# Seven block products in place of eight in the first layer of three expert visits

## The chip, the cores and the metric

The kernel runs on one core of one Trainium2 chip. The metric is the device time of one execution in microseconds (us). The core has a matrix engine (TensorE, PE), VectorE (DVE), ScalarE (ACT), GpSimd (POOL) and the queue of SyncE (SP) that issues the transfers.

## The reference

```python
def reference(**kwargs):                                   # shortened
    attn = top32_attention(q, k, v)                        # 2 x 8 heads x 576 x 64
    x = attn.transpose(0, 2, 1, 3).reshape(1152, 512)
    # first mixture: every token goes through every expert
    logits = x @ w_gate; P = np.exp(logits - logits.max())
    for _ in range(8):                                     # Sinkhorn
        P /= P.sum(1, keepdims=True) + 1e-09
        P /= P.sum(0, keepdims=True) + 1e-09
        P *= N / E
    for e in range(8):
        out += P[:, e:e + 1] * (np.maximum(x @ w1[e], 0.0) @ w2[e])   # w1: 512 x 1024, w2: 1024 x 512
    # second mixture: each token goes to the expert of its largest logit, capacity 288
    return moe2(out, ...)
```

All inputs and the output are float32. The change concerns the first mixture alone, and in it the product `x @ w1[e]` of some tokens and experts.

## The kernel before

The 1152 tokens lie transposed in SBUF (`xt`, 512 features in four chunks `d` of 128 partitions, one column for a token) and are cut into nine tiles of 128. Every float32 operand of a fast matmul is split in two parts: a rounding (`h`) that ScalarE makes and a remainder (`l`), a difference that VectorE or GpSimd makes. A product is then three matmuls: h by h, h by l, l by h.

A *visit* `(e, t0, t1)` takes expert `e` over the tiles `t0` to `t1 - 1`. It goes through eight *hidden blocks* of 128 hidden units. For each, `weights()` loads a block of w1 (`ra`) and of w2 (`rb`) and splits both (L975 on ScalarE; the remainder at L981 on GpSimd in early visits, at L978 on VectorE in late ones). The first layer (L1041) is 12 matmuls with as many columns as the visit has tokens, summed in one PSUM bank; `parts()` makes the Relu and its rounding (L989, ScalarE) and the remainder (L991, VectorE); the second layer (L1153) is three matmuls of 512 columns for each tile, summed over the eight hidden blocks in one bank a tile. At the end of a visit an early one parks its tiles in DRAM (L1142, L1144), and a late one multiplies them by the Sinkhorn weights and adds them to `acc` (`combine()`, L1175 and L1178). `restore()` brings the parked ones back (L1188) through the three buffers `ys` and `yt`, and adds them in the same way.

The visits in `EARLY` are interleaved with attention. When attention is over, `turn_over()` frees its memory and makes the late buffers; the job is called `gate` (its copy is L359). From there `sinkhorn()` runs: eight rounds, each with four small VectorE operations on rows (L1212 to L1215: a reduce, a TENSOR_SCALAR, a reciprocal, a TENSOR_TENSOR), a TensorE matmul that sums over partitions (L1225), and four on columns (L1218 to L1221, of the same kinds). The visits in `LATE` follow: three of 512 columns (experts 5, 6 and 7 over tiles 2 to 5), one of 256 columns (expert 2 over tiles 4 and 5), and eight *whole* ones of 384 columns (tiles 6 to 8). A whole visit makes all eight hidden blocks first and then the second layer tile by tile, with its own buffers for hidden blocks (`h_last`, cut from `ff`) and for w2 (`w2_last`, cut from `v`). Meanwhile tiles whose sum is finished are routed for the second mixture (`route_all()`, L1706 to L1781).

The order on each engine is fixed when the program is built. `Order` keeps a clock for each engine; every job has a rank and an estimated cost, and an engine takes the job that can start first, the lowest rank among those that can start within 0.02 us. Each engine then runs its list in that order and waits, in it, for what a job depends on. The ranks that matter here are:

```python
R = -2000                            # sinkhorn, every engine
rank - 1.5, rank                     # PE: first layer, second layer (rank = 1000 + unit)
-1000 + k * 0.001                    # ACT, DVE: Relu, remainder of a hidden block
-500 + rank, -100 + rank             # ACT: rounding of weights; DVE or POOL: remainder
-50, 10                              # restored outputs: DVE add, SP load
```

There are eight PSUM banks; in the late part five belong to the pool `psm` (hidden blocks and output tiles) and three to `psa`.

Of the kernel before, what the change touches and what calls it, by code (L numbers as in the profile page):

```python
# [219 lines left out]
class Net:  # L220
# [971 lines left out]
    def sinkhorn(self):  # L1192
# [39 lines left out]
        self.restore()  # L1232

    def made_late(self, mem):
# [9 lines left out]
        n = 4 * self.cap  # L1244
        cut = [v[:, i * n:(i + 1) * n].rearrange("p (d c) -> p d c", d=4) for i in range(4)]
        self.over = [cut[:2], cut[2:]]
        self.rest = v[:, 4 * n:]
        flat = self.ff.rearrange("p a b -> p (a b)")
        cut = [flat[:, i * self.DM:(i + 1) * self.DM] for i in range(12)]
        self.end_ = [cut[i:i + 2] for i in range(0, 12, 2)]  # L1250
# [579 lines left out]
```

## Time and profile before

| | |
|---|---|
| median of 3 runs | 1176.47 us (1176.34 to 1177.87) |
| profiled execution | 1177.07 us, span of its instructions 1175.2 us |
| PE, DVE, ACT, POOL busy in the span | 1151.5, 907.2, 729.5, 440.5 us |
| granted TensorE clock | 0.998 of 2.4 GHz |
| HBM traffic | 165 GB/s over the span |

The span runs from the first to the last instruction. Matmuls are pipelined, so two that follow each other overlap in the records, and the pace is read from starts, not from durations. An engine's waits are put down to what ended last before it went on.

### The profile page before, as it was taken

How to read it: one execution, taken by the hardware profiler on the slowest of the kernel's cores; microseconds unless marked ns; L12 is line 12 of the kernel's file. 1: busy time of each engine (PE TensorE's matmuls, PEld its weight loads, DVE VectorE, ACT ScalarE, POOL GpSimd, SP SyncE). 2: the span in 40 equal slices, each digit the busy share in tenths (PEclk: the TensorE clock that was granted, in tenths of full speed). 3: DMA queues.
4: the chain of work that ended last, by engine and by line, in shares of the span. 5: the costliest groups of instructions: out<-in, count | busy, mean ns of one | idle time of the engine just before them, and what ended most of it. 6: DMA issues, size and time to landing. Idle time of an engine off the chain costs nothing.

```text
span 1175.2 us, 20867 instructions
## 1 busy us (share of the span) xinstructions
PE 1151.5 (98%) x6607; PEld 1005.3 (86%) x6607; DVE 907.2 (77%) x2178; ACT 729.5 (62%) x1731; POOL 440.5 (37%) x403
## 2 busy tenths in 40 slices
PE   8999999999999999999999999999999999999997
PEld 5877888888889888888888888989999999898886
DVE  7998999999999999998655567844555555568882
ACT  7666889888788877768543334543334444258882
POOL 5466877777556744547500000100000000016541
PEclk9999999999999999999999999999999999999999
DMA  5467666655444655536555555643444444279980
GB/s 141 110 173 204 200 182 186 190 167 156 138 134 111 201 164 148 164 109 187 153 184 175 161 171 155 204 135 114 130 125 144 144 131 136 75 238 358 344 273 23
DMA packets 243607, 195.08 MB, mean 166 GB/s; under 512 B 67551, under 2 KB 186335, under 8 KB 243488
## 3 DMA queue, kind: packets, MB, share of 16 engines
q1 hardware_dynamic: 241232, 188.78, 53.8%
q0 software_dynamic: 1648, 4.73, 1.0%
q8 instruction: 54, 0.88, 0.3%
q14 instruction: 65, 0.53, 0.2%
q10 hardware_dynamic: 608, 0.15, 0.1%
HBM read 172.87 MB, written 21.33 MB: 165 GB/s over the span
## 4 chain that ended last, share of the span: by engine, by line
PE 54%; DVE 31%; ACT 6%; issue 5%; DMA 2%; POOL 1%; SPq 0%; POOLq 0%; DVEq 0%; ACTq 0%
PE yp L1041 14%; PE yp L1153 12%; PE tp L1153 8%; DVE wk L773 7%; PE tp L1041 6%; DVE m L775 6%; DVE e L784 3%; DVE hl L991 2%; DVE m L769 2%; PE yp L1372 2%; DVE wk L719 2%; DVE etl L830 2%; DVE m L721 1%; PE tp L264 1%; PE tp L1388 1%
## 5 line engine op out<-in xcount | busy, mean ns | idle before, releaser
L1781 POOL DMA_INDIRECT disp<-acc,idx x9 | 10.3, 1141 | 436.7 <-DVE run L1777 436.7
L981 POOL TENSOR_TENSOR w0l<-ra,w0h 128x512 fp32r<-128x512 f32 x104 | 134.8, 1296 | 95.0 <-ACT w0h L975 88.3
L981 POOL TENSOR_TENSOR w1l<-rb,w1h 128x512 fp32r<-128x512 f32 x104 | 134.7, 1296 | 49.8 <-ACT w1h L975 45.6
L975 ACT ACTIVATE w0h<-ra 128x512 fp32r<-128x512 f32 x211 | 131.9, 626 | 0.0
L775 DVE MAX8 m<-wk 128x8 f32<-128x576 f32 x168 | 125.0, 751 | 1.1
L975 ACT ACTIVATE w1h<-rb 128x512 fp32r<-128x512 f32 x148 | 93.3, 630 | 52.3 <-PE yp L1153 41.3
L1041 PE MATMUL yp<-xh,w0h 128*128 128x256 f32 (+2 forms) x528 | 107.2, 325 | 0.3 <-DVE hl L991 0.2
L1041 PE MATMUL yp<-xl,w0h 128*128 128x256 f32 (+2 forms) x528 | 106.7, 324 | 0.0
L1041 PE MATMUL yp<-xh,w0l 128*128 128x256 f32 (+2 forms) x528 | 106.6, 323 | 0.0
L1153 PE MATMUL yp<-w1h,hh 128*128 128x512 f32 x240 | 98.0, 408 | 0.4 <-DVE hl L991 0.4
L989 ACT ACTIVATE hh<-yp 128x256 fp32r<-128x256 f32 (+3 forms) x113 | 49.6, 439 | 76.3 <-PE yp L1041 60.0
L1041 PEld LDWEIGHTS yp<-xh,w0h 128*128 128x128 f32 x528 | 87.7, 188 | 10.1 <-DVE hl L991 1.6
L1153 PE MATMUL yp<-w1l,hh 128*128 128x512 f32 x240 | 94.2, 393 | 0.0
L1153 PE MATMUL yp<-w1h,hl 128*128 128x512 f32 x240 | 94.1, 392 | 0.0
L975 ACT ACTIVATE v<-rb 128x512 fp32r<-128x512 f32 x65 | 40.5, 629 | 79.5 <-PE yp L1153 41.8
L991 DVE SCALAR_TENSOR_TENSOR hl<-yp,hh 128x256 fp32r<-128x256 f32 (+3 forms) x113 | 55.2, 488 | 44.2 <-ACT hh L989 43.7
L1041 PEld LDWEIGHTS yp<-xh,w0l 128*128 128x128 f32 x528 | 85.1, 189 | 3.8
L1041 PEld LDWEIGHTS yp<-xl,w0h 128*128 128x128 f32 x528 | 85.0, 189 | 3.9
L1153 PE MATMUL yp<-v,f 128*128 128x512 f32 x360 | 84.4, 391 | 0.0
L773 DVE MATCH_REPLACE8 wk<-m,wk 128x576 f32<-128x576 f32 x112 | 83.2, 743 | 0.4
L1153 PEld LDWEIGHTS yp<-v,f 128*128 128x128 f32 x360 | 67.2, 188 | 13.5
L978 DVE TENSOR_TENSOR w0l<-ra,w0h 128x512 fp32r<-128x512 f32 x107 | 73.5, 687 | 0.4
(555 smaller groups left out, 3026.2 us busy)
## 6 DMA issues: line engine op xcount, KB each, us to landing
rb<-in_moe_w_dram SPq DMA_DIRECT2D x248, 256.0 KB, 3.0
ra<-in_moe_w_dram SPq DMA_DIRECT2D x245, 256.0 KB, 3.1
acc<-in_moe_w_dram SPq DMA_DIRECT2D x67, 256.0 KB, 6.0
y<-ys SPq DMA_DIRECT2D x33, 256.0 KB, 2.4
ys<-y SPq DMA_DIRECT2D x23, 256.0 KB, 3.0
vr<-in_v_dram SPq DMA_DIRECT2D x40, 128.0 KB, 2.8
disp<-z SPq DMA_DIRECT2D x6, 771.0 KB, 5.0
qg<-in_q_dram SPq DMA_DIRECT2D x63, 64.0 KB, 2.6
```

The lines of the kernel that those rows point to most:

```text
L719: j = self.job("DVE", r, 0.73, lambda i=i: nc.vector.match_replace(wk.t, m.t[:, i], flat() if i == 0 else wk.t, LOW), deps=[j], take=[wk] ...
L769: j = j0 = self.job("DVE", r, 0.66, lambda: nc.vector.max(m.t[:, 0], flat()), deps=got, take=[m])
L773: j = self.job("DVE", r, 0.73, lambda i=i: nc.vector.match_replace(wk.t, m.t[:, i], flat() if i == 0 else wk.t, LOW), deps=[j], take=[wk] ...
L775: j = self.job("DVE", r, 0.66, lambda i=i: nc.vector.max(m.t[:, i + 1], wk.t), deps=[j], use=[wk] if i == 2 else [])
L784: masks.append(self.job("DVE", r, t_dve(288) + 0.08, lambda half=half, p=p: nc.vector.scalar_tensor_tensor(e.t[:, half * 288:(half + 1) * ...
L975: jh = self.job("ACT", -500 + rank, t_act(512, True), lambda r=r, w=w: nc.scalar.activation(w.t[0], r.t, AF.Copy), deps=[j], take=[w])
L978: jl = self.job("DVE", -100 + rank, t_dve(512, True), lambda r=r, w=w: nc.vector.tensor_sub(w.t[1], r.t, w.t[0].bitcast(F32)), deps=[jh], ...
L981: jl = self.job("POOL", -100 + rank if k > 8 * NATIVE + 4 else FIRST - 3, t_pool(512), lambda r=r, w=w: nc.gpsimd.tensor_sub(w.t[1], r.t, ...
L989: jh = self.job("ACT", -1000 + k * 0.001, t_act(b - a), lambda: nc.scalar.activation(h.t[0][:, a:b], p.t[:, :b - a], AF.Relu), deps=deps, ...
L991: jl = self.job("DVE", -1000 + k * 0.001, t_dve(b - a), lambda: nc.vector.scalar_tensor_tensor(h.t[1][:, a:b], p.t[:, :b - a], 0.0, h.t[0] ...
L1041: nc.tensor.matmul(p.t[:, :b - a], w1[0].t[i][:, d, :], self.xt[s][:, d, c0 + a:c0 + b], start=m == 0 and d == 0, stop=m == 2 and d == 3)
L1153: nc.tensor.matmul(y[t].t, h.t[i][:, c:c + 128], w2[0].t[s], start=f == 0 and m == 0, stop=f == last and m == 2)
```

## The change

The three visits of experts 5, 6 and 7 over tiles 2 to 5 become `visit_seven()`. It takes hidden blocks in pairs. The first layer of a pair is a product of a 2 by 2 arrangement of weight blocks (two hidden blocks by two halves of the 512 features) with a 2 by 2 arrangement of tokens (two halves of the features by two halves of 256 columns). Strassen's scheme, in Winograd's form, makes the four results from seven block products. Each product is 6 matmuls of 256 columns (three for the two parts, by two chunks). The sums of weight blocks S1 to S4 are made by GpSimd for every pair, then rounded by ScalarE (L975's form) and given a remainder by VectorE. The sums of token blocks are made once, in `halves()`, by ten GpSimd operations of 512 columns, four ScalarE roundings and four GpSimd remainders. The products go to four banks; banks that are summed further are copied in between by ScalarE (`snap`), and four VectorE operations add or subtract a bank and a copy; Relu and remainder then read the copy in SBUF.

The visit of expert 2 over tiles 4 and 5 is moved ahead of these three, and `restore()` is set up after it. The buffers of the whole visits (`ff`, `v`) are made only when the last of the three is done (`made_last()`), in the memory of the buffers of `visit_seven()` (`mid`).

```diff
--- before.py
+++ after.py
@@ -25,7 +25,8 @@
 WITH = 3
 FILL = 390.0
 EARLY = [(0, 0, 1), (1, 0, 1)] + [(e, 0, 2) for e in range(2, 8)] + [(0, 1, 4), (1, 1, 4), (2, 2, 4), (3, 2, 6), (4, 2, 6), (0, 4, 6), (1, 4, 6)]
-LATE = [(5, 2, 6), (6, 2, 6), (7, 2, 6), (2, 4, 6)] + [(e, 6, 9) for e in (2, 3, 4, 5, 6, 7, 0, 1)]
+SEVEN = [(5, 2, 6), (6, 2, 6), (7, 2, 6)]
+LATE = [(2, 4, 6)] + SEVEN + [(e, 6, 9) for e in (2, 3, 4, 5, 6, 7, 0, 1)]
 ALONE = 16
 FIRST = 16
 ROWS = 16
@@ -1008,8 +1009,14 @@
                 self.visit(*v, early=True)
 
     def late_one(self):
+        self.halves()
         for v in LATE[:-1]:
+            if v in SEVEN:
+                self.visit_seven(*v)
+                continue
             self.visit(*v, whole=v[2] - v[1] == 3)
+            if v == LATE[0]:
+                self.restore()
         self.visit(*LATE[-1], whole=True)
         seen = sorted((e, t) for e, a, b in EARLY + LATE for t in range(a, b))
         assert seen == [(e, t) for e in range(self.E) for t in range(self.NT)]
+    def halves(self):
+
+        nc, c0, n = self.nc, 256, 256
+        b = self.sums_.box()
+        x = [[[self.xt[s][:, 2 * i:2 * i + 2, c0 + k * n:c0 + k * n + n] for k in (0, 1)] for i in (0, 1)] for s in (0, 1)]
+        self.cut_x = x
+        f = lambda s, a, z: x[s][a][z].bitcast(F32)
+
+        made = [d for t in range(2, 6) for d in self.xdone[t]] + [self.gate]
...
+        def step(eng, fn, deps, take=()):
+            e = nc.vector if eng == "DVE" else nc.gpsimd
+            cost = t_dve(512, True) if eng == "DVE" else t_pool(512)
+            return self.job(eng, -99.0, cost, lambda: fn(e), deps=deps, take=take, use=[b])
...
+        j = step("POOL", sub(r[0], g(0, 0, 1), g(0, 0, 0)), made, take=[b])
+        j3 = step("POOL", sub(r[2], g(0, 1, 1), g(0, 0, 1)), made + [j])
+        j3 = step("POOL", sub(r[3], g(1, 1, 1), g(1, 0, 1)), [j3])
+        j3 = step("POOL", add(r[2], r[2], r[3]), [j3])
+        j = step("POOL", sub(r[4], g(1, 0, 1), g(1, 0, 0)), [j])
+        j1 = step("POOL", add(r[0], r[0], r[4]), [j])
+        j = step("POOL", sub(r[1], g(0, 1, 1), r[0]), [j1])
+        j2 = step("POOL", add(r[1], r[1], g(1, 1, 1)), [j])
+        j = step("POOL", sub(r[3], r[1], g(0, 1, 0)), [j2, j3])
+        j4 = step("POOL", sub(r[3], r[3], g(1, 1, 0)), [j])
+        self.halved = []
+        for i, j in enumerate((j1, j2, j3, j4)):
+            jh = self.job("ACT", -600, t_act(512, True), lambda i=i: nc.scalar.activation(self.tt[0][:, i], room(i), AF.Copy),
+                          deps=[j], use=[b])
+            jl = self.job("POOL", -99.5, t_pool(512), lambda i=i: nc.gpsimd.tensor_sub(
+                self.tt[1][:, i], room(i), self.tt[0][:, i].bitcast(F32)), deps=[jh], use=[b])
+            self.halved += [jh, jl]
+
+    def visit_seven(self, e, t0, t1):
+
+        nc, fb, y, n = self.nc, self.F // 128, {}, 256
+        banks = [self.psm.box(), self.psm.box()]
+        for f in range(0, fb, 2):
+            pair = f // 2
...
+            k, rank = self.unit, 1000 + self.unit
+            self.unit += 2
+            raw, loads, w2 = [], [], []
+            for m in range(2):
+                r, cut = self.r7.box(), slice((f + m) * 128, (f + m + 1) * 128)
+                loads.append(self.job("SP", 20 + 0.001 * (k + m), 0.45, lambda r=r, cut=cut: nc.sync.dma_start(
+                    r.t, self.w11[e, :, cut].rearrange("(c p) n -> p c n", p=128)), take=[r], lag=1.35))
+                raw.append(r)
+            ra, rb = raw
+            a, q = self.seven.box(), self.sums_.box()
+            R = -98 + 0.001 * k
+            def pool(fn, deps, take=(), ra=ra, rb=rb, a=a, q=q):
+                return self.job("POOL", R, t_pool(256), lambda: fn(nc.gpsimd, ra.t, rb.t, q.t), deps=deps, take=take, use=[ra, rb, q])
+            g = self.gate
+            js = pool(lambda v, x, z, o: v.tensor_add(o[:, 0], z[:, 0:2], z[:, 2:4]), loads + [g], [q])
+            js = pool(lambda v, x, z, o: v.tensor_sub(o[:, 1], o[:, 0], x[:, 0:2]), [js])
+            js = pool(lambda v, x, z, o: v.tensor_sub(o[:, 2], x[:, 0:2], z[:, 0:2]), [js])
+            js = pool(lambda v, x, z, o: v.tensor_sub(o[:, 3], x[:, 2:4], o[:, 1]), [js])
+            fine = []
...
+                    (3, 7, lambda q=q: q.t, [js], q))):
+                w = (hi - lo) * 256
+                jh = self.job("ACT", -500 + 0.001 * k, t_act(w, True), lambda a=a, lo=lo, hi=hi, part=part: nc.scalar.activation(
+                    a.t[0][:, lo:hi], part(), AF.Copy), deps=deps, take=[] if m else [a], use=[a, box])
+                jl = self.job("DVE", -100 + 0.001 * k, t_dve(w, True), lambda a=a, lo=lo, hi=hi, part=part: nc.vector.tensor_sub(
+                    a.t[1][:, lo:hi], part(), a.t[0][:, lo:hi].bitcast(F32)), deps=[jh], use=[a, box])
+                fine.append([jh, jl])
...
+            p = [banks[pair]] + [self.psa.box() for _ in range(3)]
+            c = [pool_.box() for pool_ in self.taken]
+            order = ((0, A11, old(0, 0), True), (2, S1, new(0), True), (1, A12, old(1, 0), True), (0, S2, new(1), False),
+                     (3, A22, new(3), True), (2, S4, old(1, 1), False), (0, S3, new(2), False))
+            snap = {0: (0, 0), 1: (2, 2), 3: (0, 1), 4: (3, 3)}
+            j, shot, ends, ready, at = None, {}, [], [], {}
+            for m, (bank, blk, mov, opens) in enumerate(order):
+                def product(bank=bank, blk=blk, mov=mov, opens=opens, p=p, a=a):
+                    for i, (u, s) in enumerate(((0, 0), (0, 1), (1, 0))):
+                        for d in range(2):
+                            nc.tensor.matmul(p[bank].t[:, :n], a.t[u][:, blk, d], mov(s, d), start=opens and i == 0 and d == 0,
+                                             stop=i == 2 and d == 1, skip_group_check=True)
+                deps = [j] + fine[0 if blk < 2 else 1 if blk == 2 else 2] + ([] if m else self.halved)
+                deps += [shot[w] for w in shot if order[w][0] == bank]
+                j = at[m] = self.job("PE", rank - 2.5, 6 * t_pe(n), product, deps=deps, take=[p[bank]] if opens else [],
+                                     use=[a, p[bank]])
+                if m in snap:
+                    b_, o_ = snap[m]
+                    shot[m] = self.job("ACT", -1010 + k * 0.001, t_act(n), lambda b_=b_, o_=o_, p=p, c=c: nc.scalar.activation(
+                        c[o_].t, p[b_].t[:, :n], AF.Copy), deps=[j], take=[c[o_]], use=[p[b_], c[o_]])
+            hs = [self.h.box(), (self.hx if pair % 2 else self.h).box()]
+            fresh = [True, True]
+            parts = [[], []]
+            for o_, b_, after, op, m, col in ((0, 1, [at[2], shot[0]], OP.add, 0, 0), (1, 2, [at[5], shot[3]], OP.add, 0, n),
+                                              (2, 0, [at[6], shot[1]], OP.add, 1, n), (3, 0, [at[6], shot[4]], OP.subtract, 1, 0)):
+                h = hs[m]
+                jc = self.job("DVE", -1010 + k * 0.001, t_dve(n), lambda o_=o_, b_=b_, op=op, p=p, c=c: nc.vector.tensor_tensor(
+                    c[o_].t, p[b_].t[:, :n], c[o_].t, op=op), deps=after, use=[p[b_], c[o_]])
+                jh = self.job("ACT", -1000 + k * 0.001, t_act(n, True), lambda o_=o_, c=c, h=h, col=col: nc.scalar.activation(
+                    h.t[0][:, col:col + n], c[o_].t, AF.Relu), deps=[jc], take=[h] if fresh[m] else [], use=[c[o_], h])
+                fresh[m] = False
+                jl = self.job("DVE", -1000 + k * 0.001, t_dve(n, True), lambda o_=o_, c=c, h=h, col=col:
+                              nc.vector.scalar_tensor_tensor(h.t[1][:, col:col + n], c[o_].t, 0.0,
+                                                             h.t[0][:, col:col + n].bitcast(F32), op0=OP.max, op1=OP.subtract),
+                              deps=[jh], use=[c[o_], h])
+                parts[m] += [jh, jl]
...
+            for m in range(2):
+                for t in range(t0, t1):
+                    self.layer2(e, t, t0, f + m, hs[m], w2[m], parts[m], y, rank + m, False)
+        if (e, t0, t1) == SEVEN[-1]:
+            self.job("X", 0, 0.0, self.made_last, deps=[j] + parts[0] + parts[1] + [self.chain[t] for t in range(t0, t1)])
...
-        self.restore()
+        self.seven, self.sums_, self.hx, self.r7 = (Pool([]) for _ in range(4))
+        self.taken = [Pool([]) for _ in range(4)]
...
-        n = LATE[-1]
-        self.ff = mem.tile([128, 16, (n[2] - n[1]) * 128], F32R, name="f")
-        self.h_last.free += [(self.o.t["X"], [self.ff[:, i], self.ff[:, i + 1]]) for i in range(0, 16, 2)]
-        v = mem.tile([128, 16 * self.DM], F32R, name="v")
-        cut = [v[:, i * self.DM:(i + 1) * self.DM] for i in range(16)]
-        self.w2_last.free += [(self.o.t["X"], cut[i:i + 2]) for i in range(0, 16, 2)]
...
+        self.mid, now = ExitStack(), self.o.t["X"]
+        a = self.space(self.mid, "mid", reuse_waits="tile")
+        for i in range(2):
+            self.seven.free.append((now, [a.tile([128, 7, 2, 128], F32R, name=f"s{x}{i}") for x in "hl"]))
+        for i in range(2):
+            self.sums_.free.append((now, a.tile([128, 4, 2, 128], F32, name=f"sums{i}")))
+        for i in range(4):
+            self.r7.free.append((now, a.tile([128, 4, 128], F32, name=f"rc{i}")))
+        self.tt = [a.tile([128, 4, 2, 256], F32R, name=f"t{x}") for x in "hl"]
+        for i, pool in enumerate(self.taken):
+            pool.free.append((now, a.tile([128, 256], F32, name=f"c{i}")))
+        self.hx.free.append((now, [a.tile([128, 512], F32R, name=f"g{x}") for x in "hl"]))
+
+    def made_last(self):
+
+        self.mid.close()
+        mem, n = self.space(self.sb, "end", reuse_waits="tile"), LATE[-1]
+        self.ff = mem.tile([128, 16, (n[2] - n[1]) * 128], F32R, name="f")
+        self.h_last.free += [(self.o.t["X"], [self.ff[:, i], self.ff[:, i + 1]]) for i in range(0, 16, 2)]
...
+        self.w2_last.free += [(self.o.t["X"], cut[i:i + 2]) for i in range(0, 16, 2)]
```

## Rows read from the trace of the kernel before

**Rows 1.** The page's engine table: busy us (share of span) and instructions.

```profile
PE 1151.5 (98%) x6607; PEld 1005.3 (86%) x6607; DVE 907.2 (77%) x2178; ACT 729.5 (62%) x1731; POOL 440.5 (37%) x403
```

**Rows 2.** Stretches: length; busy us (instructions) per engine; granted clock, DMA share, GB/s.

```profile
570.00:580.00 10.00, 8.13 (x53) 7.20 (x51) 7.83 (x23) 4.44 (x9) 5.84 (x5) 1.00 0.51 148
...
660.00:690.00 30.00, 30.00 (x134) 24.84 (x133) 19.17 (x30) 9.46 (x18) 0.00 (x0) 1.00 0.55 172
...
740.00:750.00 10.00, 10.00 (x69) 8.90 (x69) 8.58 (x36) 5.95 (x15) 1.23 (x1) 1.00 0.89 272
```

**Rows 3.** Chain that ended last, pieces in order: start us, length us, engine, tile, line.

```profile
713.75 2.72 PE yp L1041 x12
...
719.19 1.43 PE yp L1041 x12
```

**Rows 4.** Timeline of TensorE: Sinkhorn matmul; start, length us, [idle before, releaser].

```profile
576.67 0.44 PE L1225 MATMUL tp<-prob,ones 128*128 128x72 f32 x2 [1.87 <-DVE prob L1215]
...
594.27 0.34 PE L1225 MATMUL tp<-prob,ones 128*128 128x72 f32 x2
...
597.72 0.33 PE L1225 MATMUL tp<-prob,ones 128*128 128x72 f32 x2
```

**Rows 5.** Timeline of VectorE, some operations; columns as in rows 4.

```profile
570.15 0.17 DVE L1213 TENSOR_SCALAR rsum<-rsum 128x9 f32<-128x9 f32 x1
...
570.61 0.23 DVE L1215 TENSOR_TENSOR prob<-prob,rsum 128x72 f32<-128x72 f32 x1
...
572.25 1.30 DVE L1219 TENSOR_SCALAR csum<-csum 128x8 f32<-128x8 f32 x1
...
574.35 0.98 DVE L1213 TENSOR_SCALAR rsum<-rsum 128x9 f32<-128x9 f32 x1
...
575.62 1.00 DVE L1215 TENSOR_TENSOR prob<-prob,rsum 128x72 f32<-128x72 f32 x1
...
580.45 1.30 DVE L1219 TENSOR_SCALAR csum<-csum 128x8 f32<-128x8 f32 x1
...
583.16 0.42 DVE L991 SCALAR_TENSOR_TENSOR hl<-yp,hh 128x256 fp32r<-128x256 f32 x1
583.49 0.68 DVE L978 TENSOR_TENSOR w0l<-ra,w0h 128x512 fp32r<-128x512 f32 x1
584.09 0.68 DVE L978 TENSOR_TENSOR w1l<-rb,w1h 128x512 fp32r<-128x512 f32 x1
...
721.50 0.73 DVE L1178 SCALAR_TENSOR_TENSOR acc<-tp,prob,acc 128x512 f32<-128x512 f32 x1
722.16 0.74 DVE L1178 SCALAR_TENSOR_TENSOR acc<-yp,prob,acc 128x512 f32<-128x512 f32 x1
```

**Rows 6.** Timeline of GpSimd, the same stretch.

```profile
574.02 1.28 POOL L981 TENSOR_TENSOR w0l<-ra,w0h 128x512 fp32r<-128x512 f32 x1 [0.51 <-ACT w0h L975]
575.26 1.27 POOL L981 TENSOR_TENSOR w1l<-rb,w1h 128x512 fp32r<-128x512 f32 x1
...
580.44 1.29 POOL L981 TENSOR_TENSOR w1l<-rb,w1h 128x512 fp32r<-128x512 f32 x1
```

**Rows 7.** Groups by line and shape: busy us, mean ns; idle before, releasers.

```profile
L981 POOL TENSOR_TENSOR w0l<-ra,w0h 128x512 fp32r<-128x512 f32 x104 | 134.8, 1296 | 95.0 <-ACT w0h L975 88.3 <-PE tp L866 2.5 <-ACT st L770 2.2
...
L975 ACT ACTIVATE w0h<-ra 128x512 fp32r<-128x512 f32 x211 | 131.9, 626 | 0.0
...
L1041 PEld LDWEIGHTS yp<-xh,w0h 128*128 128x128 f32 x528 | 87.7, 188 | 10.1 <-DVE hl L991 1.6
...
L989 ACT ACTIVATE hh<-yp 128x256 fp32r<-128x256 f32 x77 | 29.3, 381 | 23.1 <-PE yp L1372 11.5 <-PE yp L1041 8.7 <-DVE w1l L978 1.6
...
L859 POOL TENSOR_TENSOR vs<-vr,vs 128x256 fp32r<-128x256 f32 x24 | 16.6, 690 | 12.5 <-ACT vs L856 11.1 <-PE tp L264 1.2
```

**Rows 8.** Groups of VectorE in 600 to 719 us: restored outputs.

```profile
L1178 DVE SCALAR_TENSOR_TENSOR acc<-ys,prob,acc 128x512 f32<-128x512 f32 x17 | 12.7, 746 | 0.0
L1178 DVE SCALAR_TENSOR_TENSOR acc<-yt,prob,acc 128x512 f32<-128x512 f32 x9 | 6.7, 746 | 0.0
```

More of the change, by code (lines that the diff above doesn't have):

```diff
@@ new lines, in visit_seven @@
+    def visit_seven(self, e, t0, t1):
[3 more added lines that the diff above has]
+            pair = f // 2
+            if pair > 1:
+                banks.append(self.psm.box())
+            k, rank = self.unit, 1000 + self.unit
[6 more added lines that the diff above has]
+                raw.append(r)
+                r, w = self.r2.box(), self.w2.box()
+                j = self.job("SP", 20 + 0.001 * (k + m), 0.45, lambda r=r, cut=cut: nc.sync.dma_start(r.t, self.w12[e, cut]),
+                             take=[r], lag=1.35)
+                jh = self.job("ACT", -500 + 0.001 * (k + m), t_act(512, True), lambda r=r, w=w: nc.scalar.activation(
+                    w.t[0], r.t, AF.Copy), deps=[j], take=[w])
+                jl = self.job("DVE", -100 + 0.001 * (k + m), t_dve(512, True), lambda r=r, w=w: nc.vector.tensor_sub(
+                    w.t[1], r.t, w.t[0].bitcast(F32)), deps=[jh], use=[r])
+                w2.append((w, jh, jl))
+            ra, rb = raw
[9 more added lines that the diff above has]
+            fine = []
+            for m, (lo, hi, part, deps, box) in enumerate((
+                    (0, 2, lambda ra=ra: ra.t.rearrange("p (m d) c -> p m d c", d=2), [loads[0]], ra),
+                    (2, 3, lambda rb=rb: rb.t[:, None, 2:4], [loads[1]], rb),
+                    (3, 7, lambda q=q: q.t, [js], q))):
[5 more added lines that the diff above has]
+                fine.append([jh, jl])
+            A11, A12, A22, S1, S2, S3, S4 = range(7)
+            x, old = self.cut_x, lambda i, z: lambda s, d: self.cut_x[s][i][z][:, d]
+            new = lambda i: lambda s, d: self.tt[s][:, i, d]
+            p = [banks[pair]] + [self.psa.box() for _ in range(3)]
[34 more added lines that the diff above has]
+                parts[m] += [jh, jl]
+            if not pair:
+                for t in range(t0, t1):
+                    y[t] = self.psm.box()
+            for m in range(2):
+                for t in range(t0, t1):
+                    self.layer2(e, t, t0, f + m, hs[m], w2[m], parts[m], y, rank + m, False)
+        if (e, t0, t1) == SEVEN[-1]:
+            self.job("X", 0, 0.0, self.made_last, deps=[j] + parts[0] + parts[1] + [self.chain[t] for t in range(t0, t1)])
@@ L1237, in more @@
             pool.free += [(self.o.t["X"], t) for _, t in other.free]
-        n = LATE[-1]
-        self.ff = mem.tile([128, 16, (n[2] - n[1]) * 128], F32R, name="f")
-        self.h_last.free += [(self.o.t["X"], [self.ff[:, i], self.ff[:, i + 1]]) for i in range(0, 16, 2)]
-        v = mem.tile([128, 16 * self.DM], F32R, name="v")
-        cut = [v[:, i * self.DM:(i + 1) * self.DM] for i in range(16)]
-        self.w2_last.free += [(self.o.t["X"], cut[i:i + 2]) for i in range(0, 16, 2)]
[L1244 to L1250, printed above, removed]
         more(self.ys, self.pool(mem, "yt", [128, self.DM], 1))
@@ L1274, in made_late @@
                    for i in range(2)]
+        self.mid, now = ExitStack(), self.o.t["X"]
[15 more added lines that the diff above has]
+        self.h_last.free += [(self.o.t["X"], [self.ff[:, i], self.ff[:, i + 1]]) for i in range(0, 16, 2)]
+        v = mem.tile([128, 16 * self.DM], F32R, name="v")
+        cut = [v[:, i * self.DM:(i + 1) * self.DM] for i in range(16)]
+        self.w2_last.free += [(self.o.t["X"], cut[i:i + 2]) for i in range(0, 16, 2)]
+        n = 4 * self.cap
+        cut = [v[:, i * n:(i + 1) * n].rearrange("p (d c) -> p d c", d=4) for i in range(4)]
+        self.over = [cut[:2], cut[2:]]
+        self.rest = v[:, 4 * n:]
+        flat = self.ff.rearrange("p a b -> p (a b)")
+        cut = [flat[:, i * self.DM:(i + 1) * self.DM] for i in range(12)]
+        self.end_ = [cut[i:i + 2] for i in range(0, 12, 2)]
     def mixture_two(self):
```

7 lines of the change are left out of this document (added).

## The prediction

> **What bounds the kernel now.** I read the engine table of the page first, then busy time by stretch, then the chain that ended last, and then the timelines of three engines around the turn from attention to the late visits. TensorE is busy 98% of the span [rows 1], so the question of every edit is whether it shortens TensorE's work or opens a hole in it. The stretches [rows 2] say where holes are: from 588 us on TensorE has none (30.00 of 30.00 us in 660 to 690, 10.00 of 10.00 in 740 to 750), and the granted clock is 1.00, that is 2.4 GHz; the one poor stretch is 570 to 580, with 8.13 of 10. In 660 to 690 VectorE is busy 19.17 of 30, ScalarE 9.46, GpSimd 0. So the three visits that change are pure TensorE time with room beside them. In the chain [rows 3] a first layer of 512 columns is a piece of 2.72 us (12 matmuls, 0.2267 each) and the next piece starts 5.44 us after it, so the second layer of a hidden block is 2.72 too; the 256-column visit that follows shows 1.43 us for 12 (0.119 each).
>
> The poor stretch is the Sinkhorn loop, a chain VectorE - TensorE - VectorE of eight rounds. Its matmul stands in TensorE's queue in a fixed place, so when VectorE is late TensorE waits: 1.87 us before the one at 576.67 [rows 4]; undisturbed, two rounds lie 3.45 us apart (594.27, 597.72). Why VectorE was late shows in its timeline beside GpSimd's [rows 5, 6]. A TENSOR_SCALAR on 9 columns takes 0.17 us at 570.15, with GpSimd idle, but 0.98 at 574.35, and a TENSOR_TENSOR on 72 columns takes 1.00 at 575.62. Each of the two ends, within 0.1 us, when the GpSimd operation that had started before it ends (574.02 plus 1.28, 575.26 plus 1.27); the same at 580.45 (1.30, against GpSimd's 580.44 plus 1.29). And between GpSimd's back-to-back operations (574.02 and 575.26, 1.24 apart) exactly one VectorE operation slipped in. So a small VectorE operation of these kinds waits out a whole running GpSimd operation.
>
> **The change, part by part.**
>
> *Fewer products.* A pair of hidden blocks had 24 matmuls of 0.2267, 5.44 us. It gets 7 products of 6 matmuls with 256 columns, 42 times 0.119 = 5.00. Saved 0.44 per pair, twelve pairs: **-5.2 us** [rows 3]. The second layers stay, so a pair is 10.44 us where it was 10.88. This is all that can be won.
>
> *Visit of expert 2 moved ahead.* The same matmuls in another place: 0 by itself. It covers, in time, the preparation of the sums of the tokens. But it now stands in the Sinkhorn loop, with two vector differences per 2.8 us of TensorE time, where the 512-column visit had two per 5.44.
>
> *Sums of the tokens (halves).* Ten GpSimd additions on 512 columns and four differences, each like the 1.296 us row [rows 7], 1.24 apart when back to back [rows 6]: 14 x 1.24 = 17.4 us of GpSimd; the four ScalarE roundings (0.63 each) lie in ScalarE's idle time (4.44 busy of 10 in 570 to 580). They become ready when attention's memory turns over, that is at the start of the Sinkhorn loop, and a planner that starts what can start puts them there at once. GpSimd already works 5.84 of the 10 us of 570 to 580 for the early visits; with these, and with the weight sums of the first two pairs behind them (8 x 0.69 = 5.5 us), it runs nearly without a gap from the turn to about 600 us. In that time each round has four VectorE operations of the waiting kinds (two TENSOR_SCALARs, two TENSOR_TENSORs). If one slips in per GpSimd boundary, a round takes at least 4 x 1.24 = 5.0 us in place of 3.45: 1.5 more, in some 5.5 rounds 8.5. The weight differences of VectorE that lie between (TENSOR_TENSOR with both inputs in SBUF, as the 72-column one) each need a boundary too: two per hidden block, six in the last three blocks of that stretch, about 0.8 each after what the loop's own wait for TensorE hides, 4.8. Off go the 1.87 that before already loses here: 11.4. The other way round: three waits (1.13 at 572.25, 0.81, and 0.77 against 0.23 undisturbed at 570.61; together 2.7) cost TensorE 1.87, or 0.69 of their length; 22 new GpSimd operations that each catch one VectorE operation for 0.9 cost 22 x 0.9 x 0.69 = 13.7, and if only half catch one, 7. I take **+10**, bounds 3 (a quarter catch one) and 14. What is queued behind each wait: VectorE's remainders of the hidden activations and weights, and behind the Sinkhorn matmul TensorE's whole queue. TensorE has no spare time later in which to make it up.
>
> The Trainium skill, page "SBUF — State Buffer", section "Who interferes with whom", states the same as a rule: a VectorE instruction with two SBUF inputs, or in a two-port mode, and a GpSimd instruction that reads SBUF exclude each other, and the second waits for the whole of the first. The rows above agree for TENSOR_TENSOR and TENSOR_SCALAR; no row here shows SCALAR_TENSOR_TENSOR, which the page includes. By the page the next term would lie at its upper bound of 4.3, and the sum at 1187.
>
> *The seven visits' other engines, per pair of 10.44 us.* VectorE by starts that lie 0.60 apart for 512 columns (583.49, 584.09) and 0.33 for 256 (583.16, 583.49), and 0.66 for the closing of a tile (721.50, 722.16) [rows 5]: weights of layer two 2 x 0.60; remainders of the seven operand blocks 0.60 + 0.33 + 1.13 (1024 columns, an estimate from the two spacings); four sums and four remainders of 256, 8 x 0.33; one closing, 0.66; restored outputs, 26 in the old stretch [rows 8], 2.2 x 0.66 = 1.4. Together 8.0. GpSimd adds four sums of 0.69 = 2.8, in which VectorE may be locked out: 10.8 at worst, against 10.44. The worst is then 0.36 x 12 = 4.3; at best nothing, as the second layer of the pair before (5.44 us) covers the chain sum, Relu, remainder. I take 1.5. ScalarE: 2 x 0.63 for layer two, 2.2 for the operands, eight copies of 0.38 [rows 7]: 6.5 of 10.44. A bank is opened again two products after its copy (1.43 us); a copy behind a 1024-column rounding (1.15, estimate) ends 1.5 after the product, so a pair loses 0 to 0.3; I take 0.04, 0.5 in all.
>
> *Buffers after the last seven visit.* The memory of the last visits' hidden blocks and second weights now comes free only when the last second layer is done, so their eight weight pairs are prepared in the first layer of the next visit, of 384 columns: 8 x 2.08 us (half way between 1.43 and 2.72) plus some 7 us of the routing's matmuls, an estimate, where before there was the 256-column visit. VectorE is at 8.58 of 10 there [rows 2]. Eight differences more, 4.8 us, have 24 us plus the 5.4 of the first tile's second layer, which uses them one after another: 0 to 4, I take 0.5.
>
> **Sum.** The profiled execution took 1177.07 (span 1175.2, 1.9 outside it): 1177.07 - 5.2 + 10 + 1.5 + 0.5 + 0.5 = 1184.4. The median of the runs is 0.6 lower; I say **1184**. A difference under 0.2% (2.4 us) can't be told from none here.
>
> **Rivals.**
>
> *It gets faster (0.24).* The lock at the turn is real but costs TensorE little, because the additions fall in rounds whose slack swallows them, or two VectorE operations slip in per boundary. If the turn costs under 2.7 us, the 5.2 win against it and the 2.5 of small terms; at 0 to 1 the time is 1172 to 1174 (lowest 1177.1 - 5.2 = 1171.9). For it: only 570 to 582 has shown the waits, and 580.45's wait of 1.13 us cost TensorE little. Against: TensorE's hole of 1.87 us with GpSimd only 58% busy.
>
> *It cancels (0.12).* The turn costs 3 to 7: 1174.5 to 1179.
>
> *VectorE becomes the bound of the seven visits as well (0.14).* All two-input operations wait and nothing overlaps: +4.3 in place of 1.5, and up to 3.5 more from the weight pairs at the end: 1187 to 1191. For it: 10.8 against 10.44. Against: the restored outputs end before the last visits, and then 9.4 is left.
>
> *256-column products run at the pace of weight loads.* LDWEIGHTS rows are 0.188 us [rows 7] against 0.119 per matmul; 42 x 0.188 = 7.9 would add 29 us. The visit at 719.19 with the same shape runs at 0.119, so I give it nothing.
>
> **How the numbers follow.** My case, the turn at 7 to 14 with small terms near what I take: 0.50, 1181 to 1189. With VectorE's case 0.64 slower, 0.12 same, 0.24 faster. The range goes down to 1172.5, which leaves out the best fifth of the faster case, and up to 1190, which leaves out most of VectorE's: under 2 in 10 together. The likeliest case alone is 1181 to 1189.
>
> **What would show it.** Right: the L1213, L1215, L1219 and L1221 rows many at about 1 us; waits of 2 us and more before TensorE's L1225; GpSimd busy over 9 of 10 from 568 to 600; the loop ending some 10 us later than 599; pairs 10.4 us apart later on. Wrong: L1225 without waits, the first seven visit starting by 612, and a span shorter by 3 to 5 us. Wrong in another way: pairs at 11 us with TensorE waiting for VectorE's remainders.

## The result and the profile after

The kernel with the change takes 1184.38 us, the kernel before 1176.78 on the same chip (medians of six runs each): ratio 1.0055, 95% interval 1.0042 to 1.0068. It is slower, by 7.6 us; 1184.0 was predicted. The profiled execution took 1185.0, with a span of 1183.2 (1175.2 before). Single executions of the kernel before, in the rounds of the experiments, range from 1175.4 to 1181.3 us, the longer ones at the lower granted clock (0.999 down to 0.994), so one profiled execution can lie up to some 4 us from the median. First the engine table, which answers to [rows 1]:

```profile
PE 1152.4 (97%) x6823; PEld 1013.9 (86%) x6823; DVE 956.2 (81%) x2262; ACT 757.7 (64%) x1819; POOL 502.4 (42%) x465
```

The total of TensorE says little: fewer columns, but the same busy time, since stretches at the lower clock, shown below, count as busy. The stretches say more (columns as in [rows 2]):

```profile
570.00:580.00 10.00, 7.17 (x45) 6.20 (x44) 9.36 (x17) 4.42 (x11) 9.75 (x9) 1.00 0.67 206
580.00:590.00 10.00, 7.31 (x38) 6.40 (x37) 9.02 (x23) 3.37 (x8) 6.34 (x6) 0.83 0.18 52
...
660.00:690.00 30.00, 30.00 (x193) 27.34 (x192) 26.12 (x47) 16.04 (x38) 10.55 (x12) 1.00 0.55 161
```

In the Sinkhorn loop GpSimd went from 5.84 to 9.75 of 10 us and TensorE lost a further microsecond in ten; between 580 and 590 the granted clock is 0.83, which no stretch shown of before had. In 660 to 690, inside the visits of seven products, VectorE has gone from 19.17 to 26.12 and TensorE still has no hole. So the loss lies in the loop. TensorE's timeline there, the loop's matmul and some of those behind it (it answers to [rows 4]):

```profile
571.85 0.41 PE L1365 MATMUL tp<-prob,ones 128*128 128x72 f32 x2 [0.95 <-DVE prob L1355]
...
576.99 0.44 PE L1365 MATMUL tp<-prob,ones 128*128 128x72 f32 x2 [1.87 <-DVE prob L1355]
...
583.45 0.49 PE L1365 MATMUL yp<-prob,ones 128*128 128x72 f32 x2 [2.69 <-DVE prob L1355]
...
584.69 0.63 PE L1293 MATMUL yp<-w1h,hh 128*128 128x512 f32 x1
585.11 0.63 PE L1293 MATMUL yp<-w1l,hh 128*128 128x512 f32 x1
...
599.16 0.44 PE L1365 MATMUL yp<-prob,ones 128*128 128x72 f32 x2 [2.83 <-DVE prob L1355]
...
606.87 0.44 PE L1365 MATMUL tp<-prob,ones 128*128 128x72 f32 x2 [1.44 <-DVE prob L1355]
...
611.22 0.44 PE L1365 MATMUL tp<-prob,ones 128*128 128x72 f32 x2 [0.34 <-DVE prob L1355]
```

Six waits, 10.1 us together, where before had two of 2.2 together. Behind the wait of 2.69 us the 512-column matmuls start 0.43 apart, not 0.23: that is the lower level of the clock, 1.2 GHz. Why VectorE was late, from its timeline and GpSimd's (they answer to [rows 5, 6]):

```profile
569.29 1.12 DVE L1353 TENSOR_SCALAR rsum<-rsum 128x9 f32<-128x9 f32 x1
...
570.69 1.01 DVE L1355 TENSOR_TENSOR prob<-prob,rsum 128x72 f32<-128x72 f32 x1
...
573.14 1.04 DVE L1361 TENSOR_TENSOR prob<-prob,csum 128x72 f32<-128x72 f32 x1
...
574.48 1.17 DVE L1353 TENSOR_SCALAR rsum<-rsum 128x9 f32<-128x9 f32 x1
...
577.19 1.44 DVE L1148 TENSOR_TENSOR sl<-rc,sh 128x512 fp32r<-128x512 f32 x1
...
580.09 1.03 DVE L1361 TENSOR_TENSOR prob<-prob,csum 128x72 f32<-128x72 f32 x1
581.04 1.49 DVE L1148 TENSOR_TENSOR sl<-rc,sh 128x256 fp32r<-128x256 f32 x1
```

```profile
569.08 1.29 POOL L982 TENSOR_TENSOR w1l<-rb,w1h 128x512 fp32r<-128x512 f32 x1
570.34 1.27 POOL L982 TENSOR_TENSOR w0l<-ra,w0h 128x512 fp32r<-128x512 f32 x1
...
572.80 1.29 POOL L1084 TENSOR_TENSOR acc<-xh 128x512 f32<-128x512 f32 x1
574.34 1.28 POOL L982 TENSOR_TENSOR w0l<-ra,w0h 128x512 fp32r<-128x512 f32 x1 [0.25 <-ACT w0h L976]
...
579.75 1.28 POOL L1084 TENSOR_TENSOR acc<-acc,sums 128x512 f32<-128x512 f32 x1
580.99 1.26 POOL L982 TENSOR_TENSOR w0l<-ra,w0h 128x512 fp32r<-128x512 f32 x1
```

The VectorE operations at 569.29, 570.69 and 574.48 end at 570.41, 571.70 and 575.65; the GpSimd operations that began before them, weight remainders of early visits that before has too, end at 570.37, 571.61 and 575.62. Behind the new work it is the same: the operations at 573.14 and 580.09 end at 574.18 and 581.12, and the token sums (L1084) that began before them at 574.09 and 581.03. It is the pattern of [rows 5, 6], now in almost every round. In what follows this waiting for a running operation of the other engine is called the lock. The rows of L1148 are new work of VectorE itself: four operand remainders of the first two pairs stand in the loop already, and the one at 581.04, held for 1.49 us, lies on the way to the wait of 2.69.

The gain shows in the chain that ended last, by the second layers of the pairs (start, length, engine, tile, line):

```profile
637.12 2.04 PE yp L1293 x9
...
741.99 2.04 PE yp L1293 x9
...
842.71 5.46 PE tp L1293 x24
```

From 637.12 to 741.99 lie ten pairs of hidden blocks: 10.49 us a pair, against 10.88 before. That is 0.39 a pair, 4.7 for twelve. The third row is a landmark for what follows: the second layer of the third whole visit (expert 4, tiles 6 to 8), the same work in all kernels here.

**One scale for all runs.** The start of the loop wanders by a microsecond between runs, with attention. So the table counts from the matmul that opens the loop (L1202 in before, L1342 in after: its maximum over partitions) to the landmark, both from the profiled execution. "Waits" are TensorE's before the loop's matmul and, from there to 1000 us, before a first layer.

| kernel | opening to landmark, us | against before | waits, us |
|---|---|---|---|
| before | 836.08 - 568.63 = 267.45 | | 2.2 |
| after | 842.71 - 567.76 = 274.95 | +7.5 | 10.1 |
| e1_order | 836.15 - 568.65 = 267.50 | 0.0 | 2.2 |
| e2_extra_pool | 846.57 - 568.56 = 278.01 | +10.6 | 8.9 |
| e3_no_token_sums | 833.21 - 567.40 = 265.81 | -1.6 | 4.1 |
| e4_psum_vectors | 832.67 - 567.17 = 265.50 | -2.0 | 3.6 |
| g1_before_psum | 832.49 - 567.71 = 264.78 | -2.7 | 0 |
| g2_write_only_pool | 840.60 - 568.30 = 272.30 | +4.8 | 4.8 |
| g3_sums_after_loop | 838.87 - 567.87 = 271.00 | +3.5 | 6.3 |
| g4_both | 836.48 - 568.90 = 267.58 | +0.1 | 3.4 |
| h3_sums_wait_for_loop | 838.38 - 568.20 = 270.18 | +2.7 | 7.0 |
| h4_wait_and_psum_vectors | 835.56 - 568.00 = 267.56 | +0.1 | 4.5 |

### The profile page after: what moved, and what is told of

Its sections match the earlier page's. It is cut to its first block, busy times and chain, and to the rows that moved or that the text cites. A ratio compares the mean times of both kernels' runs of the same rounds, so it can differ in the third digit from the quotient of the medians.

```text
span 1183.2 us, 21535 instructions
## 1 busy us (share of the span) xinstructions
PE 1152.4 (97%) x6823; PEld 1013.9 (86%) x6823; DVE 956.2 (81%) x2262; ACT 757.7 (64%) x1819; POOL 502.4 (42%) x465
## 4 chain that ended last, share of the span: by engine, by line
PE 53%; DVE 33%; ACT 6%; issue 5%; POOL 2%; DMA 1%; SPq 0%; POOLq 0%; DVEq 0%; ACTq 0%
PE yp L1293 13%; PE yp L1048 8%; DVE wk L774 7%; PE tp L1293 7%; DVE m L776 6%; PE tp L1048 6%; PE tp L1164 4%; DVE e L785 4%; DVE hl L992 2%; DVE m L770 2%; PE tp L1529 2%; DVE wk L720 2%; PE yp L1529 2%; DVE etl L831 2%; PE yp L1545 2%
## 5 line engine op out<-in xcount | busy, mean ns | idle before, releaser
L976 ACT ACTIVATE w0h<-ra 128x512 fp32r<-128x512 f32 x187 | 116.7, 626 | 8.4 <-PE tp L1048 8.4
L976 ACT ACTIVATE w1h<-rb 128x512 fp32r<-128x512 f32 x124 | 78.0, 629 | 12.8 <-PE yp L1293 4.5
L1048 PE MATMUL yp<-xh,w0h 128*128 128x256 f32 (+2 forms) x436 | 82.6, 311 | 0.3 <-DVE hl L992 0.3
L1048 PE MATMUL yp<-xh,w0l 128*128 128x256 f32 (+2 forms) x436 | 82.2, 310 | 0.0
L1048 PE MATMUL yp<-xl,w0h 128*128 128x256 f32 (+2 forms) x436 | 81.8, 309 | 0.0
L1048 PEld LDWEIGHTS yp<-xh,w0h 128*128 128x128 f32 x436 | 70.9, 190 | 6.7 <-DVE hl L992 1.6
L1048 PEld LDWEIGHTS yp<-xh,w0l 128*128 128x128 f32 x436 | 68.3, 191 | 0.2
L1048 PEld LDWEIGHTS yp<-xl,w0h 128*128 128x128 f32 x436 | 67.7, 189 | 0.2
L794 ACT ACTIVATE e<-e,st 128x576 f32<-128x576 f32 x56 | 43.5, 776 | 22.0 <-DVE st L793 21.5
L1048 PE MATMUL tp<-xl,w0h 128*128 128x384 f32 (+2 forms) x268 | 57.4, 335 | 0.0
```

The costliest lines, as they stand in the source:

```text
L794: jn = self.job("ACT", r, t_act(576, True, 1), lambda: nc.scalar.activation(e.t, e.t, AF.Copy, scale=st.t[:, 4:5]), deps=[ji], use=[st])
L976: jh = self.job("ACT", -500 + rank, t_act(512, True), lambda r=r, w=w: nc.scalar.activation(w.t[0], r.t, AF.Copy), deps=[j], take=[w])
L1048: nc.tensor.matmul(p.t[:, :b - a], w1[0].t[i][:, d, :], self.xt[s][:, d, c0 + a:c0 + b], start=m == 0 and d == 0, stop=m == 2 and d == 3)
```

## Experiments

Two theories stood at the start: that the loss is GpSimd's new work holding VectorE in the loop (the prediction's), and that it is the new order, with expert 2's small visit in the loop and the late buffers.

**e1_order**: the order and the late buffers of after, but plain visits.

```
 def late_one(self):
-    self.halves()
...
-            self.visit_seven(*v)
+            self.visit(*v)
```

> The changed kernel's order and buffers, with the plain visits of eight products in place of the seven-product ones; nothing of the sums is made. Lock theory (the loss is VectorE waiting behind GpSimd at the turn): no GpSimd work is added, so the order alone costs little, 0 to +2.5 us against before, 1177 to 1179; TensorE's Sinkhorn matmul waits no more than before (2.2 us in all). Rival, the order and the late buffers are the loss: +8 to +12, 1185 to 1189.

1178.38 against 1177.9 us, ratio 1.0003 (0.9991 to 1.0016). TensorE's waits, of the view of waits by line:

```profile
PE tp L1366 <- DVE prob L1356: 2.2, 2, 1.9
```

The order and the buffers cost nothing that shows, here or on the common scale; the rival falls.

**e2_extra_pool**: the kernel before, with 14 GpSimd differences of 512 columns that nothing uses, from the start of the loop.

```
+for i in range(14):
+    j = self.job("POOL", -99.0, t_pool(512), lambda i=i: nc.gpsimd.tensor_sub(
+        self.acc[:, 6 + i % 3, :512]..., x[i % 4], x[(i + 1) % 4]), deps=made + [j])
```

> The kernel before with one thing added: 14 GpSimd differences of 512 columns, as many as the token sums need, started at the turn; their results are overwritten later, nothing reads them. Lock theory: the Sinkhorn rounds stretch from 3.4 to about 5 us while they run, TensorE waits before its Sinkhorn matmul for 4 to 8 us in all, and the time is 1181 to 1185. Rival (the loss sits in the products, the order or the late buffers): GpSimd is otherwise idle there, so 0, 1176 to 1177.5.

1189.53, ratio 1.0097 (1.0079 to 1.0115): 11.6 us slower, more than expected. TensorE's timeline, VectorE's and GpSimd's:

```profile
586.67 0.44 PE L1234 MATMUL tp<-prob,ones 128*128 128x72 f32 x2 [2.56 <-DVE prob L1224]
...
594.98 0.70 PE L1234 MATMUL tp<-prob,ones 128*128 128x72 f32 x2 [2.50 <-DVE prob L1224]
```

```profile
588.24 1.76 DVE L978 TENSOR_TENSOR w1l<-rb,w1h 128x512 fp32r<-128x512 f32 x1
```

```profile
587.72 1.73 POOL L1015 TENSOR_TENSOR acc<-xl 128x512 f32<-128x512 f32 x1
589.41 1.72 POOL L1015 TENSOR_TENSOR acc<-xl,xh 128x512 f32<-128x512 f32 x1
```

GpSimd's work alone makes a loss of after's kind. The lock holds both ways: VectorE's difference of 0.68 us takes 1.76, and GpSimd's of 1.29 takes 1.73 when one slips in. On the common scale the loss is 3.9 us more than the added waits (10.6 against 6.7), and most of that is the clock: 0.90 in 580 to 590 and 0.76 in 590 to 600, at most 3.4 us.

**e3_no_token_sums**: after without the 14 operations on the tokens.

```
-        j = step("POOL", sub(r[0], g(0, 0, 1), g(0, 0, 0)), made, take=[b])
...
+            jh = self.job("ACT", -600, ..., nc.scalar.activation(self.tt[0][:, i], f(0, i % 2, i // 2), AF.Copy), ...)
```

> The changed kernel without the token sums: the 14 GpSimd operations are left out and the products that need sums read rounded parts of the tokens themselves, copied by ScalarE, so those first layers are not the reference's. Lock theory: most waits of the turn go; 8 of 22 added GpSimd operations (the weight sums of the first two pairs) and their waits stay: 7 to 9 us faster than the changed kernel, 1175 to 1177.5. Rival, the loss sits in the seven-product visits: no more than 2 us faster, 1182 or more.

The second mixture is routed otherwise here (370.1 us from the landmark to the end, 338.8 to 340.5 in before, after, e1, e4 and g1), so its 1202.88 us don't compare; the landmark does. It comes 9.1 us sooner than in after by the table, 1.6 below before. Of 12.2 us (below) some 9 go with the token sums. The other 3.1 are 1.9 us of waits more than before's and 1.2 that stay open; how they are shared between the weight sums and VectorE's new remainders (L1148 in after), which both stay in the loop here, no run shows.

**e4_psum_vectors**: after, with the loop's row and column vectors in a PSUM bank, so that its TENSOR_SCALAR and TENSOR_TENSOR read at most one operand from SBUF. **g1_before_psum** does the same to the kernel before.

```
-        s, r, q = self.sk, self.rsum, self.csum
+        s, hold = self.sk, self.psa.box()
+        r = lambda: hold.t[:, :3 * NT].rearrange("p (a t) -> p a t", a=3)
+        q = lambda: hold.t[:, 64:64 + 3 * E].rearrange("p (a e) -> p a e", a=3)
```

> The changed kernel with the small vectors of the Sinkhorn rounds (row and column sums, their reciprocals) in a PSUM bank in place of SBUF; GpSimd's work is all there. Lock theory: the four operations of a round now have at most one SBUF input and run in 0.2 to 0.3 us whatever GpSimd does; only the weight differences still wait; 7 to 10 us faster than the changed kernel, 1174 to 1177.5. Rival, VectorE is late because of the weight differences that stand in front of the rounds, or because a busy GpSimd slows every VectorE operation: at most 3 us faster, 1181 or more.

> The kernel before with the Sinkhorn vectors in a PSUM bank and nothing else changed. Lock theory: the four operations that waited for GpSimd before the change (1.1, 0.8, 0.8 and 1.1 us) stop waiting, TensorE's 2.2 us before its Sinkhorn matmul go, 1174 to 1175.5 against 1176 to 1178 of before. Rival, the gain of the PSUM vectors in the changed kernel came from something else than the waits (another order, shorter operations): the same time as before, or a gain as large as there (8 us).

e4: 1175.81, ratio 0.998 (0.9967 to 0.9993), 8.6 us below after. g1: 1174.78, ratio 0.9972 (0.9961 to 0.9983). The 8.6 us compare medians of two rounds; on the common scale it is 9.5. VectorE's timeline in e4, then 567 to 614 by stretch in e4 and in g1:

```profile
568.70 0.18 DVE L1355 TENSOR_SCALAR tp<-tp 128x9 f32<-128x9 f32 x1
...
575.43 0.22 DVE L1354 TENSOR_REDUCE tp<-prob 128x9 f32<-128x72 f32 x1
575.69 0.17 DVE L1355 TENSOR_SCALAR tp<-tp 128x9 f32<-128x9 f32 x1
575.90 0.23 DVE L1356 RECIPROCAL tp<-tp 128x9 f32<-128x9 f32 x1
576.16 0.23 DVE L1357 TENSOR_TENSOR prob<-prob,tp 128x72 f32<-128x72 f32 x1
...
588.11 1.83 DVE L979 TENSOR_TENSOR w0l<-ra,w0h 128x512 fp32r<-128x512 f32 x1
```

```profile
567.00:614.00 47.00, 43.20 (x279) 38.46 (x280) 41.16 (x103) 25.29 (x51) 43.27 (x36) 1.00 0.67 204
```

```profile
567.00:614.00 47.00, 46.50 (x246) 39.85 (x246) 29.88 (x97) 22.03 (x41) 9.67 (x12) 1.00 0.59 179
```

GpSimd is busy 43.27 of 47 us and the loop's operations run at their undisturbed 0.17 and 0.23. With that, 6.5 of the 10.1 us of TensorE's waits are gone, and no stretch at 1.2 GHz is left in the loop: the cause of the greater part of the waits is shown. But the weight differences between them still stretch, to 1.83, and TensorE still waits 3.6. On the common scale e4 is 0.7 us behind g1 although its pairs win 4.7: the scheme brings nothing that could be seen even here. The two medians can't be told apart.

**g2_write_only_pool**: as e2, with memsets of the same time (they write SBUF and read nothing).

```
-    nc.gpsimd.tensor_sub(...)
+    nc.gpsimd.memset(self.acc[:, 6:9, :455], 0.0)
```

> The kernel before with 14 GpSimd fills of 1365 columns at the turn, each about as long as a difference (1.3 us) but reading nothing. If a running GpSimd operation of any kind holds VectorE: as with the 14 differences, 1187 to 1191. If only the path by which GpSimd reads is contended: the 72-column TENSOR_TENSORs and the weight differences run at 0.23 and 0.69, the 9-column TENSOR_SCALARs may still wait, and the time is 1177 to 1182. If neither waits: 1176 to 1178.

1181.81, ratio 1.0032 (1.002 to 1.0043): less than half of e2's loss. VectorE's timeline while the memsets run (582.51 to 598.04):

```profile
581.31 2.48 DVE L1226 TENSOR_SCALAR csum<-csum 128x8 f32<-128x8 f32 x1
...
584.06 0.23 DVE L1228 TENSOR_TENSOR prob<-prob,csum 128x72 f32<-128x72 f32 x1
...
585.85 0.68 DVE L978 TENSOR_TENSOR w0l<-ra,w0h 128x512 fp32r<-128x512 f32 x1
...
591.93 0.94 DVE L1226 TENSOR_SCALAR csum<-csum 128x8 f32<-128x8 f32 x1
```

TENSOR_TENSOR is free, TENSOR_SCALAR still waits. So it matters that GpSimd reads for the one kind and not for the other. The page "SBUF — State Buffer" of the Trainium skill, section "Who interferes with whom", parts them in the same way: two SBUF inputs meet GpSimd's reads alone, a two-port mode meets GpSimd altogether. Whether these TENSOR_SCALARs run in such a mode no trace here shows.

**g3_sums_after_loop** makes expert 5's visit plain (eight pairs in place of twelve) and tells the planner to put the sums behind the loop; **g4_both** adds the PSUM vectors.

```
-SEVEN = [(5, 2, 6), (6, 2, 6), (7, 2, 6)]
+SEVEN = [(6, 2, 6), (7, 2, 6)]
...
-        made = [...] + [self.gate]
+        made = [...] + [self.mixed]
...
-            g = self.gate
+            g = self.mixed
```

> The changed kernel with its GpSimd work (token sums and weight sums) released by the end of the Sinkhorn loop in place of the turn, and the visit of expert 5 left plain so that there is TensorE work to cover them; experts 6 and 7 keep the seven products. Lock theory: the turn is as in the kernel before (waits 2.2 us in all), eight pairs save 0.39 each, 3.1: 1173 to 1175. Rival, GpSimd's sums cost wherever they stand, because VectorE's weight differences wait for them in the plain visits too: 1177 to 1183.

> The sums after the loop and the Sinkhorn vectors in PSUM together. Lock theory: also the 2.2 us of the kernel before go: 1170.5 to 1172.5. Rival, the two mend the same waits: no better than the better one of the two alone, 1173 to 1175.5.

1180.64, ratio 1.0026 (1.0017 to 1.0035), and 1176.19, ratio 0.9985 (0.9976 to 0.9994): both misses of the theory; g3 falls into its rival's range, g4 above both. GpSimd's timeline in g3:

```profile
584.21 1.28 POOL L1084 TENSOR_TENSOR acc<-xh 128x512 f32<-128x512 f32 x1
...
589.88 2.51 POOL L1084 TENSOR_TENSOR acc<-acc,sums 128x512 f32<-128x512 f32 x2
613.72 2.53 POOL L1101 TENSOR_TENSOR tl<-acc,th 128x512 fp32r<-128x512 f32 x2 [21.33 <-ACT th L1099]
```

The edit did not do what it says. The sums use nothing of the loop's, so the dependency is an order in the plan and no wait on the chip, and GpSimd ran ahead at 584.21 into the loop. So these two say little on what the sums cost behind it.

**h3_sums_wait_for_loop** and **h4_wait_and_psum_vectors**: as g3 and g4, but GpSimd first copies a few elements that the loop's last step writes, and so truly waits.

```
+        j = step("POOL", lambda e: e.tensor_copy(self.acc[:, 6, :self.E], self.prob[:, 0]), made, take=[b])
-        j = step("POOL", sub(r[0], g(0, 0, 1), g(0, 0, 0)), made, take=[b])
+        j = step("POOL", sub(r[0], g(0, 0, 1), g(0, 0, 0)), [j])
```

> As g3_sums_after_loop (the visit of expert 5 plain, two visits with seven products), but GpSimd's first instruction of the token sums now copies nine columns of prob, so that it truly waits for the Sinkhorn loop's last VectorE step; this puts one small copy more on GpSimd. Theory (the sums cost time only while TensorE waits for each step of VectorE, that is in the loop): TensorE's waits before the loop's matmul go back to the 2.2 us of the kernel before, the eight pairs of seven products give back 8 x 0.39 = 3.1 us, and some 1 us is lost where TensorE once waits for a weight remainder (1.05 at 627 in g3_sums_after_loop): 1174 to 1176. Rival (the sums cost about the same wherever they stand, since VectorE's weight remainders of the plain visits wait for them too): 1178 to 1182, with TensorE waits before L1048 of 3 us or more between 600 and 640.

> As h3_sums_wait_for_loop, with the Sinkhorn vectors in PSUM as in g4_both. Theory: no TensorE wait of 0.3 us or more before the loop's matmul; 1174.8 of g1_before_psum less 3.1 for the eight pairs, plus some 1 us at the weight remainders: 1171.5 to 1173.5, the shortest of all kernels here. Rival (the sums cost the same wherever they stand): 1175.5 to 1179.

1181.02, ratio 1.003 (1.0019 to 1.0041), and 1177.91, ratio 0.9999 (0.9987 to 1.0011). Both times lie in the rival's range, against my theory. GpSimd, VectorE and TensorE in h4:

```profile
599.19 0.59 POOL L1087 COPY acc<-prob 128x8 f32<-128x8 f32 x1 [18.30 <-DVE prob L1364]
599.75 1.18 POOL L1137 TENSOR_TENSOR sums<-rc 128x256 f32<-128x256 f32 x1
```

```profile
614.37 1.78 DVE L979 TENSOR_TENSOR w0l<-ra,w0h 128x512 fp32r<-128x512 f32 x1
...
631.79 1.47 DVE L1149 TENSOR_TENSOR sl<-sums,sh 128x1024 fp32r<-128x1024 f32 x1 [1.72 <-ACT sh L1147]
633.18 1.21 DVE L979 TENSOR_TENSOR w0l<-ra,w0h 128x512 fp32r<-128x512 f32 x1
634.32 0.68 DVE L992 SCALAR_TENSOR_TENSOR hl<-tp,hh 128x512 fp32r<-128x512 f32 x1
```

```profile
621.70 1.19 PE L1048 MATMUL tp<-xh,w0h 128*128 128x512 f32 x4 [1.55 <-DVE hl L992]
...
635.05 1.20 PE L1048 MATMUL tp<-xh,w0h 128*128 128x512 f32 x4 [2.18 <-DVE hl L992]
```

The sums now start at 599.75, behind the loop, and the waits with them: the plain visit's weight differences take up to 1.83 us in place of 0.68, and TensorE waits before its first layers. The rival named the held remainders alone; before the wait of 2.18 us there is more: VectorE, which takes its list in order, stood idle 1.72 us for the rounding of a pair's weight sums (631.79), and the remainder that TensorE needed (634.32) stood behind it. Against g1, eight pairs should give 3.1; h4 lies 2.8 above g1, so the sums and what hangs on them cost 5.9 there. In e4 they cost 5.4 in the loop (0.7 above g1, with 4.7 won). In both places tried, in the loop and right behind it, they cost more than the products save, in e4 by no more than single executions scatter. A later place was not tried.

## Why the prediction was right, point by point

- **The turn: +10 predicted (bounds 3 to 14), 12.2 measured** (7.5 on the common scale and the 4.7 won by the pairs). The mechanism, VectorE held in the loop by GpSimd's new work, is shown by e2 (such work alone makes the loss), e4 (with the loop's operations off the lock most of it goes) and e1 (order and buffers add nothing). The size was put together otherwise: 7.9 us of waits more than before, and 3.2 us of clock, which the prediction had not priced. Behind the waits of 2.69 and 2.83 us, a stretch each runs at 1.2 GHz; by starts, six 512-column matmuls and some first-layer ones each time, 1.6 us more than at 2.4 GHz. That share varies between executions (mean granted clock 0.993 to 0.997 in the six of after, 0.994 to 0.999 in those of before). The sum also put all of VectorE's new operand remainders into the visits; four of them stood in the loop. What they add is not measured apart; e2, which has none, waits 8.9 us all the same. Some 1.1 us are left, as in the other kernels with twelve such pairs (e3 1.2, e4 1.3, by the same count: distance, plus 4.7, less the waits more than before's 2.2); where they go stays open.
- **Fewer products: -5.2 predicted, -4.7 measured.** The products run at 0.119 us as taken; a pair takes 10.49, not 10.44.
- **VectorE in the seven visits, +1.5, ScalarE, +0.5, and the late buffers, +0.5: none of them shows.** After 614 us TensorE waits nowhere before 1000. VectorE is busy 26.12 of 30, or 9.1 of a pair's 10.49: above the 8.0 of the sum, below the worst case. It is held there too, also in a SCALAR_TENSOR_TENSOR of two SBUF operands (L1318 at 652.68 takes 1.22 us beside GpSimd, 0.75 in before), which the prediction had no row for; but TensorE does not feel it, and the upper bound of 4.3 did not come. The late buffers are e1's zero. These 2.5 us too many stand against the 2.2 too few at the turn, and that the total came out within 0.4 us owes something to this.
- **The rest.** The span grew by 8.0: 7.5 to the landmark, 0.9 less before the loop, 1.4 more after the landmark. From the landmark to the end of the span before, e1 and e4 take 338.8 to 339.1 us, g1 and after 340.5. The 1.4 are the clock once more, at the same work in all five, small matmuls of the routing, with no wait of TensorE; five microseconds of it in after, then in before:

```profile
1030.00:1035.00 5.00, 5.00 (x31) 4.78 (x31) 2.52 (x16) 0.39 (x2) 0.40 (x1) 0.66 0.14 54
```

```profile
1022.00:1027.00 5.00, 5.00 (x45) 4.86 (x44) 3.77 (x23) 1.30 (x4) 0.97 (x1) 1.00 0.14 53
```

  At 0.66 that is up to 1.7 us. Since g1 shows it too (0.66 in 1020 to 1025) and e4 does not, it is no effect of the change that could be shown.
- **The rivals.** "It gets faster" needed a turn of less than 2.7 us; "it cancels", 3 to 7; 12.2 lies above both. VectorE as bound of the visits and the pace of weight loads: TensorE without a wait at 10.49 a pair speaks against both. Of the signs named, the GpSimd share "over 9 of 10 from 568 to 600" held in 570 to 580 alone (6.34 in 580 to 590, where GpSimd waits for rounded weights); the loop's last matmul came at 611.22, 13.5 us behind before's [rows 4], where some 10 was named.

## What to carry to other kernels

Fewer matmuls are paid for where the operands are made: ask at which moment the added GpSimd work runs, and which VectorE operations with two SBUF operands, or which TENSOR_SCALARs, stand on TensorE's path in that moment. A short serial VectorE chain can be taken off the lock by keeping its small vectors in PSUM; here that alone, on the kernel before, gave as short a time as any version (1174.78 us). A dependency that exists only in the plan's order does not hold an engine back on the chip; to move work behind an event, make it read what the event writes.
